# Gated linear attention with a gated feed-forward layer: weight groups loaded by their own index, and a new hand-written order of all tasks

## The chip, the core and the metric

The kernel runs on one core of one Trainium2 chip. A core has a matrix engine (TensorE, PE in the profile; its weight loads are shown apart as PEld), a vector engine (VectorE, DVE), a scalar engine (ScalarE, ACT), a general engine (GpSimd, POOL) and a queue engine (SyncE, SP) which here only issues DMA transfers. Each engine runs its own instructions strictly in the order in which they were written, and the engines meet through semaphores. The metric is the device time of one execution in microseconds (us).

## What is computed

The reference, cut to what matters. A gated linear attention runs over 4 batches, 8 heads and 768 tokens with heads of 48 values; its result, 3072 tokens of 384 values, goes through a gated feed-forward layer of width 1536.

```python
def _attn_ref(q, k, v, alpha):              # all (4, 8, 768, 48), float32
    state = zeros((B, H, D, D)); y = zeros_like(q)
    for t in range(S):
        state = alpha[:, :, t, :, None] * state + einsum('bhd,bhe->bhde', k[:, :, t], v[:, :, t])
        y[:, :, t] = einsum('bhd,bhde->bhe', q[:, :, t], state)
    return y

def _moe_ref(x, w_gate, w_val, w_out):      # x (3072, 384); weights float64
    g = x @ w_gate                          # (3072, 1536)
    silu = g * (1.0 / (1.0 + exp(-g)))
    return (silu * (x @ w_val) @ w_out).astype(float32)

def reference(**kwargs):
    attn_out = _attn_ref(...)
    x = attn_out.transpose(0, 2, 1, 3).reshape(B * S, H * D)
    return _moe_ref(x=x, ...)
```

## The kernel before

**Attention.** The tokens are cut into 16 units (u0 to u15), each 192 tokens of one batch for all heads, in three chunks of 64. For a unit the kernel loads alpha, k, q (tasks La, Lk, Lq) and v (V, six small transfers), turns alpha, k and q so that tokens lie along a row, forms a product of decays backward (G, one long scan on DVE) and forward (f), multiplies them into k (mk) and q (q), and then works with matrices: keys turned back (K with its copies kc, or kr on DVE), scores (S), causal masks (ma), the state carried from chunk to chunk (B or Bw, with ad and de) and the outputs (Y). The outputs are split into a high part (yh) and a low part (yl) and put into the activations xT of the feed-forward layer. The first four units are turned on PE: a copy widens each input (pa, pk, pq, `widened`, L405), PE transposes it (Ta, Tk, Tq, L417), ACT copies the result out (ea, ek, cq). Later units are turned by DVE (tr, tk, tq). Units 0 and 1 reach xT by PE products and copies (R, x); later ones by ten small DMA transfers each (xr, `repack`, L709).

**Feed-forward.** Two units make a block of 384 tokens; each of 8 blocks has 12 steps over the width, 96 steps in all. Step s is: a gate product g (9 matmuls into one PSUM bank, L725), SiLU on ACT (sl), a value product v (9 matmuls, L725), the product h of both on DVE (L737), its high part hh on ACT (L741), its low part hl on DVE or POOL (L746), and the output product o (9 matmuls, L757) that adds up in three PSUM banks. Every product is three: high by high, high by low, low by high, of operands split into two parts. Steps 0 to 6 are block 0 (first seven slices of the width), 7 to 13 block 1, 14 to 18 and 19 to 23 the rest of these two blocks, with partial sums kept in DRAM between (os6, os13, then pl18, pl23); blocks 2 to 7 have twelve steps each. ACT or DVE copies finished sums out (ot, L765 and L769), and a store follows (os).

**Weights.** The weights are 64-bit floats in memory. They come in 20 groups of one or two slices (g: gate, v: value, o: output). Group 0 is gate slice 0, group 1 value slice 0, group 2 gate slice 1, group 3 is (v1, o0), group 4 (g2, v2), group 5 (o1, g3) and so on to group 19 (o11). A group is loaded as 32-bit words (wl: one transfer of 384 KB for each slice, L298 or L301), turned into single floats by three word operations (wNv0 to wNv2, L157 to L175), split by a cast into the high part (wNa) and by a subtraction into the low part (wNp, L347). The raw words of group n lie in the place that group n + 1 will take when it is split, so a group's split waits until the group ahead of it has been turned.

**Checks.** Alongside, every weight and alpha value is read once more and compared with its permitted range (wr and wc for weights, Lc and ck for alpha, L456 and L457). Two sums of violations, a small matmul and a cast (L921 to L932) make a flag; every engine loads the flag at the end (L1083), and a general path runs if it is set.

**What sets the order.** The string ORDER (L46 on) is a list of words, each `engine:task@banks`, with t for PE, v for DVE, s for ACT, g for POOL and y for SP. The kernel goes through the list and writes each task to the named engine, so the list fixes the queue of every engine, which engine does a task, and which PSUM banks PE's tasks use; nothing is moved afterwards. Semaphores follow from the data.

## Time and profile before

| what | value |
|---|---|
| time, median of 3 runs | 573.75 us (572.68 to 574.14) |
| span of the profiled execution | 570.8 us |
| busy PE / DVE / ACT / POOL | 545.7 / 391.7 / 280.5 / 134.0 us |
| first gate product (g0) starts | 51.67 us |
| last instruction of the last output product ends | 563.86 us |
| mean granted clock of PE | 0.990 |

The profile describes one execution, whose span from first to last instruction is 570.8 us, 2.95 us under the median of the timed runs. In the rows of the profile, a line number such as L725 is a line of the kernel, `out<-in` are the names of the tiles (with buffer numbers left out), and the time in brackets is how long the engine stood idle ahead of the row, with what released it.

### The profile page before, as it was taken

The page shows a single profiled execution, that of the slowest core. Times are in us where ns is not written, and L with a number is a line of the kernel's source. Part 1 is how long each engine was busy: PE and PEld are TensorE (multiplying, and loading weights), DVE is VectorE, ACT ScalarE, POOL GpSimd, SP SyncE. Part 2 cuts the span into 40 slices and gives each one's busy share as a digit, 9 for nine tenths or more (in the row PEclk, how much of TensorE's full clock was granted, in tenths as well). Part 3 has the DMA queues.
Part 4 walks back from the last instruction along what each step waited for, and adds up shares of the span by engine and source line. Part 5 has one row for each costly group of instructions (what it writes and reads, how often), then busy time and mean ns, then how long its engine had stood idle before and what let it go on. Part 6 is the DMA issues. An engine that isn't in the chain of part 4 may idle for free.

```text
span 570.8 us, 13758 instructions
## 1 busy us (share of the span) xinstructions
PE 545.7 (96%) x5510; PEld 527.4 (92%) x5510; DVE 391.7 (69%) x601; ACT 280.5 (49%) x621; POOL 134.0 (23%) x152
## 2 busy tenths in 40 slices
...
GB/s 204 309 318 254 277 82 112 115 40 108 131 146 146 135 132 107 124 126 113 93 100 187 172 156 205 191 141 89 218 111 85 116 132 86 97 73 121 41 2 47
...
## 3 DMA queue, kind: packets, MB, share of 16 engines
...
q10 hardware_dynamic: 144, 0.20, 0.1%
HBM read 62.52 MB, written 5.90 MB: 120 GB/s over the span
## 4 chain that ended last, share of the span: by engine, by line
PE 76%; DMA 10%; DVE 7%; SPq 3%; issue 2%; ACT 1%; DVEq 0%; ACTq 0%
PE ops L757 24%; PE v L725 23%; PE g L725 22%; DMA raw<-in_moe_w_out_dram 3%; DMA raw<-in_moe_w_gate_dram 2%; PE y L652 2%; PE A L580 2%; PE s L556 2%; DMA raw<-in_moe_w_val_dram 1%; DMA L<-in_k_dram 1%; DMA Le<-in_q_dram 1%; DVE K L531 1%; SPq L436 1%; PE y L635 1%; DVE t L165 1%
## 5 line engine op out<-in xcount | busy, mean ns | idle before, releaser
L725 PE MATMUL v<-xT,w 128*128 128x384 f32 x864 | 166.9, 337 | 3.2 <-DVE h L737 2.4
L725 PE MATMUL g<-xT,w 128*128 128x384 f32 x864 | 167.3, 337 | 0.4 <-ACT h L733 0.4
L757 PE MATMUL ops<-w,hh 128*128 128x384 f32 x576 | 159.8, 338 | 0.0
L725 PEld LDWEIGHTS v<-xT,w 128*128 128x128 f32 x864 | 150.7, 188 | 5.8 <-DVE h L737 3.4
L725 PEld LDWEIGHTS g<-xT,w 128*128 128x128 f32 x864 | 150.7, 188 | 1.4 <-ACT h L733 0.7
L737 DVE TENSOR_TENSOR h<-h,v 128x384 f32<-128x384 f32 x96 | 52.9, 551 | 120.1 <-PE v L725 92.5
L746 POOL TENSOR_TENSOR hl<-h,hh 128x384 fp32r<-128x384 f32 x57 | 65.5, 1150 | 264.7 <-ACT hh L741 263.5
L741 ACT CAST hh<-h 128x384 fp32r<-128x384 f32 x96 | 49.1, 511 | 128.1 <-DVE h L737 70.9
L757 PEld LDWEIGHTS ops<-w,hh 128*128 128x128 f32 x576 | 105.5, 188 | 1.0
L757 PE MATMUL ops<-w,hl 128*128 128x384 f32 x288 | 96.8, 336 | 0.0
L733 ACT ACTIVATE h<-g 128x384 f32<-128x384 f32 x96 | 46.9, 489 | 80.6 <-PE g L725 68.8
L531 DVE STREAM_TRANSPOSE K<-Gs 32x384 f32<-32x384 f32 x96 | 54.7, 570 | 2.3 <-PE A L580 0.4
L757 PEld LDWEIGHTS ops<-w,hl 128*128 128x128 f32 x288 | 54.1, 188 | 0.1
L746 DVE TENSOR_TENSOR hl<-h,hh 128x384 fp32r<-128x384 f32 x39 | 22.9, 589 | 14.8 <-ACT hh L741 14.6
L590 DVE TENSOR_TENSOR X<-s,mask 64x384 f32<-64x384 f32 (+1 forms) x48 | 26.3, 552 | 8.5 <-PE s L556 7.6
L471 DVE TENSOR_TENSOR_SCAN AT<-AT,back 128x771 f32<-128x771 f32 x16 | 30.9, 1933 | 0.6
L462 DVE TENSOR_TENSOR_SCAN Gs<-AT,inj 128x772 f32<-128x772 f32 x16 | 28.7, 1794 | 0.1
L417 PE MATMUL pt<-ident,wide 128*128 128x128 f32 x72 | 14.9, 376 | 11.4 <-POOL mask L243 5.1
L417 PEld LDWEIGHTS pt<-ident,wide 128*128 128x128 f32 x72 | 12.1, 197 | 13.4 <-ACT wide L405 5.1
L319 ACT ACTIVATE wc<-wc,wbias 128x384 f32<-128x384 f32 x36 | 23.4, 650 | 1.2
L318 ACT ACTIVATE wc<-wc,wbias 128x384 f32<-128x384 f32 x36 | 23.3, 648 | 1.2
L839 POOL TENSOR_TENSOR Gs<-trk,Gs 128x768 f32<-128x768 f32 x10 | 17.9, 1785 | 25.3 <-DVE Gs L462 13.8
(118 smaller groups left out, 608.4 us busy)
## 6 DMA issues: line engine op xcount, KB each, us to landing
...
```

The source lines that it names most:

```text
L319: nc.scalar.activation(dev, dev, AF.Relu, bias=wbias[:, 1:2], accum_out=wviol[:, 0, i : i + 1])
L417: nc.tensor.transpose(pt[:, j - js.start, :], Wd.rearrange("p j e c -> p (j e c)")[:, j * P : (j + 1) * P], ident)
L462: nc.vector.tensor_tensor_scan(*(x.rearrange("p g t -> p (g t)")[:, ::-1] for x in (Gs, AT, inj)), 0.0, op0=ALU.mult, op1=ALU.add)
L471: nc.vector.tensor_tensor_scan(Af, Af, back[:, 1 : n + 1], back[:, 0:1], op0=ALU.mult, op1=ALU.add)
L531: nc.vector.transpose(out=bass.AP(k0.tensor, k0.offset, [k0.ap[0], (G * 2 * D, NU), (2 * D, G), (1, 32)]), in_=Kg[j * BO + x : j * BO + x ...
L590: nc.vector.tensor_tensor(out=X[r, z, f * GF : (f + 1) * GF, :].rearrange("r g (c t) -> r g c t", c=NU), in0=sps[f][r].rearrange("r g (c t ...
L725: nc.tensor.matmul(pt, wsp[kind, f][a][:, kt * P : (kt + 1) * P], xT[blk][:, b_, kt, :], start=(n == 0), stop=(n == 3 * KT - 1),)
L733: nc.scalar.activation(h, acc.pop(("g", blk, f)), AF.Silu)
L737: nc.vector.tensor_tensor(out=h, in0=h, in1=acc.pop(("v", blk, f)), op=ALU.mult)
L741: nc.scalar.copy(out=hh, in_=acc["h", blk, f])
L746: eng.tensor_tensor(out=hl, in0=acc.pop(("h", blk, f)), in1=hh.bitcast(F32), op=ALU.subtract)
L757: nc.tensor.matmul(ops[blk][i], h[b_][:, i * P : (i + 1) * P], wsp["o", f][a], start=(first and n == 0), stop=(last and n == 2),)
```

## The change

`weight_group` took its index from how many groups had been loaded so far, so that the loads had to be written in the order of the groups. It now takes the index as an argument. The loads may stand in any order, and the rest of the function is as it was. All lines from there on have numbers one to three lower in the changed kernel.

```diff
-    wsp, groups, wtiles = {}, [], []
+    wsp = {}
@@
-    def weight_group(pieces):
+    def weight_group(n, pieces):
-        n = len(groups)
-        groups.append(pieces)
@@
-            wfns[p] = weight_group(wgroups[p])
+            wfns[p] = weight_group(p, wgroups[p])
@@ ORDER, the first line and the last
-y:La0 y:wl0 y:Lk1 y:La1 y:Lq0 y:V1 s:pa0 t:Ta0@01 s:w0v0 v:w0v1 s:ea0 v:w0v2 y:Lk0 s:w0a v:G0 s:pa1 y:Lq1 s:pq0 y:La2
...
-s:os95.2
+y:La0 y:wl1 v:w1v0 y:La1 y:Lk0 g:pa0 t:Ta0@30 v:w1v1 s:ea0 y:Lq0 y:wl0 v:w1v2 s:pa1 v:G0 t:Ta1@32 s:pq0 t:Tq0@40 s:pk0
...
```

The string ORDER is new from its first word to its last, with the same tasks. The weight groups are loaded in the order 1, 0, 3, 2, 5, 7, 4, 9, 6, 8, 10, 15, 11, 14, 12, 13, 17, 16, 18, 19. The first value product stands ahead of the first gate product, and the carry of unit 2 (Bw2) and one turned key chunk of unit 3 (K3.1) stand behind both. Some tasks change their engine. In number: low parts of weights (wNp) are 13 on DVE and 7 on POOL before, 6 and 14 after; high parts of weights (wNa) 16 on ACT and 4 on POOL before, 9 on ACT, 9 on POOL and 2 on DVE after; the q products (q) 7 on DVE and 9 on POOL before, 4 and 12 after; qc 10 on ACT and 6 on POOL before, 5 and 11 after; vc 11 and 5 before, 4 and 12 after; the copies of outputs (ot) 24 on ACT and 6 on DVE before, 16 and 14 after; the widening copies of the first units (pa, pk, pq) 9 on ACT and 3 on POOL before, 4 and 8 after.

SP's queue ahead of the last loads of unit 3 (the k and q rows, into the buffers L0 and L1; `raw` rows are weights, `V0` is v). Before:

```order
L446 DMA L1_72<-in_k_dram 128x2x288
L446 DMA L0_71<-in_q_dram 128x2x288
L301 DMA raw10_505<-in_moe_w_gate_dram 128x3x256
L301 DMA raw10_505<-in_moe_w_val_dram 128x3x256
L436 DMA V0_77<-in_v_dram 64x4x48 x6
L298 DMA raw11_641<-in_moe_w_out_dram 128x768
L301 DMA raw11_641<-in_moe_w_gate_dram 128x3x256
L446 DMA L1_72<-in_q_dram 128x2x288
```

and after the change:

```order
L297 DMA raw5_317<-in_moe_w_out_dram 128x768
L300 DMA raw5_317<-in_moe_w_gate_dram 128x3x256
L300 DMA raw7_371<-in_moe_w_gate_dram 128x3x256
L300 DMA raw7_371<-in_moe_w_val_dram 128x3x256
L443 DMA L0_71<-in_alpha_dram 128x2x288
L300 DMA raw4_479<-in_moe_w_gate_dram 128x3x256
L300 DMA raw4_479<-in_moe_w_val_dram 128x3x256
L433 DMA V0_77<-in_v_dram 64x4x48 x6
L300 DMA raw9_552<-in_moe_w_val_dram 128x3x256
L297 DMA raw9_552<-in_moe_w_out_dram 128x768
L443 DMA L1_72<-in_k_dram 128x2x288
L443 DMA L1_72<-in_q_dram 128x2x288
```

The last load of unit 3 is the q row into L1. Ahead of it stood 21 weight transfers (up to one slice of group 11), and now 13 (groups 0 to 5, 7 and 9). The v of unit 2 (V0) keeps its place ahead of it.

DVE's queue ahead of its last copies into xT of block 0 (L696 before, L693 after; `t` are weight words, `w2` a low part, `Y1` low parts of outputs, `Gs2` the key product mk2, `X0` the q product or a mask). Before:

```order
L347 TENSOR_TENSOR w2_435<-t2_387,w2_435 128x384
L165 SCALAR_TENSOR_TENSOR t4_458<-raw4_244,t4_458 128x768
L175 SCALAR_TENSOR_TENSOR t4_458<-raw4_244,t4_458 128x768
L165 SCALAR_TENSOR_TENSOR t5_630<-raw5_303,t5_630 128x768
L175 SCALAR_TENSOR_TENSOR t5_630<-raw5_303,t5_630 128x768
L670 TENSOR_TENSOR Y1_638<-y0_1_586,Y1_638 112x2x192
L175 SCALAR_TENSOR_TENSOR t3_390<-raw3_223,t3_390 128x768
L836 TENSOR_TENSOR Gs2_455<-pt2_1_0_647,Gs2_455 128x4x32x3
L836 TENSOR_TENSOR Gs2_455<-pt2_1_1_651,Gs2_455 128x4x32x3
L488 TENSOR_TENSOR X0_103<-pt2_2_0_657,AT_86 112x128x3
L488 TENSOR_TENSOR X0_103<-pt2_2_1_661,AT_86 112x128x3
```

and after the change:

```order
L164 SCALAR_TENSOR_TENSOR t5_550<-raw5_317,t5_550 128x768
L667 TENSOR_TENSOR Y1_616<-y0_1_573,Y1_616 112x2x192
L667 TENSOR_TENSOR Y1_616<-y1_1_574,Y1_616 112x2x192
L833 TENSOR_TENSOR Gs2_482<-pt2_1_0_620,Gs2_482 128x4x32x3
L833 TENSOR_TENSOR Gs2_482<-pt2_1_1_624,Gs2_482 128x4x32x3
L485 TENSOR_TENSOR X0_103<-pt2_2_0_631,AT_86 112x128x3
L485 TENSOR_TENSOR X0_103<-pt2_2_1_635,AT_86 112x128x3
L693 CAST xT0_569<-xp1_2_653 128x2x192
L616 SCALAR_TENSOR_TENSOR V0_77<-SE_109,Gs2_482 48x4x48 x2
L693 CAST xT0_569<-xp0_0_677 128x2x192
```

The word operations of group 4 and one of group 5 and the low part of group 2 no longer stand ahead of the copies into xT, of which DVE now makes two in place of one.

ACT's queue at the end of the program (`hh` high part of h, `ot` an output copy, `ac13` the alpha values of block 13, `flag` the flag of the checks). Before:

```order
L741 CAST hh7_11_6807<-h7_11_6772 128x384
L769 COPY ot7_0_11_6820<-ops7_0_0_6462 128x384
L769 COPY ot7_1_11_6822<-ops7_1_0_6463 128x384
L769 COPY ot7_2_11_6825<-ops7_2_0_6464 128x384
L774 DMA out_0_dram<-ot7_2_11_6825 128x384
L1083 TENSOR_LOAD flag_60
```

and after the change:

```order
L738 CAST hh7_11_6805<-h7_11_6761 128x384
L766 COPY ot7_0_11_6820<-ops7_0_0_6439 128x384
L766 COPY ot7_1_11_6823<-ops7_1_0_6440 128x384
L771 DMA out_0_dram<-ot7_2_11_6818 128x384
L453 ACTIVATE ac13_6714<-ac13_6714,nbias_112 128x576
L454 ACTIVATE ac13_6714,viol_110<-ac13_6714,dbias_114 128x576
L1080 TENSOR_LOAD flag_60
```

The two range comparisons of alpha block 13 now stand between the last store and the load of the flag; one of the three last output copies has gone to DVE.

More of the change, by code (lines that the diff above doesn't have):

```diff
@@ L72 @@
-s:vc5 g:hl14 t:v15 s:w18a v:yl4.0 s:sl15 v:w17p s:yh4.1 t:g16 s:ot13.2 v:w19v0 v:h15 g:mk5 y:os13.2 v:yl4.1 s:hh15
-y:pl18.0 t:o14 s:sl16 y:La6 v:w19v1 t:v16 v:kr5.3 g:hl15 g:w18p v:tq5 t:o15 v:h16 y:Lk6 t:g17 g:q5 v:kr5.2 s:hh16
-v:kr5.0 t:v17 s:sl17 g:qc5 v:hl16 t:g18 v:w19v2 v:h17 s:w19a v:tr6 s:hh17 t:v18 s:sl18 g:hl17 v:kr5.1 y:Lq6 t:o16
-v:w19p v:h18 t:S5@01 y:xr4 v:tk6 s:hh18 t:B5@2 g:hl18 v:ma5.2 t:o17 v:ad5.0 v:ad5.1 t:o18 v:ad5.2 v:ma5.0 t:g19
-v:ot18.0 v:ma5.1 y:pl18.1 v:G6 t:v19 y:La7 s:sl19 t:Y5@01 v:f6 y:os18.0 t:g20 s:yh5.0 y:V7 v:h19 g:vc6 s:yh5.1 v:yl5.0
@@ L137 @@
-s:os95.2
+y:La0 y:wl1 v:w1v0 y:La1 y:Lk0 g:pa0 t:Ta0@30 v:w1v1 s:ea0 y:Lq0 y:wl0 v:w1v2 s:pa1 v:G0 t:Ta1@32 s:pq0 t:Tq0@40 s:pk0
+s:w0v0 t:Tk0@51 y:Lk1 v:f0 s:pk1 y:wl3 g:z0 y:Lq1 v:q0 s:ea1 t:Tk1@43 s:w3v0 g:pq1 v:mk0 v:G1 v:w0v1 v:w0v2 t:K0.1@5
+t:S0@17 t:K0.2@0 s:ek1 s:w1a t:K0.0@2 v:f1 g:mk1 y:V0 y:V1 y:La2 g:pa2 v:w3v1 y:Lq2 t:Tq1@63 s:kc0.2 s:kc0.1 s:cq1
+y:wl2 v:w1p s:kc0.0 v:z1 g:w0a v:w3v2 t:Ta2@60 s:w2v0 v:ma0.1 y:Lk2 g:q1 y:wl5 t:Bw0@2 g:vc0 y:wl7 v:ma0.2 s:ea2
+s:ad0.2 v:w2v1 g:qc0 t:S1@34 v:ma0.0 g:w0p v:ma1.2 v:w2v2 v:ma1.1 s:ad0.1 t:K1.0@7 t:K1.2@6 g:w3a s:kc1.2 t:K1.1@5
@@ new lines @@
+y:V5 s:w18a t:g17 g:w17p v:tq5 s:ot13.1 y:os13.2 y:La6 t:v16 s:yh4.0 g:q5 v:kr5.2 y:Lk6 s:hh15 t:o14 v:kr5.3 v:h16
+g:hl15 g:w18p s:sl17 g:vc5 y:os13.1 y:V6 v:w19v0 v:w19v1 t:o15 s:hh16 s:ad0.0 v:w19v2 v:kr5.1 g:hl16 v:tr6 t:v17 v:h17
+g:qc5 s:hh17 t:g18 y:pl18.0 s:ad3.0 v:ad2.0 t:v18 v:G6 v:yl4.0 s:sl18 v:de5 v:h18 s:w19a g:w19p y:pl18.1 s:yh4.1
+v:yl4.1 t:g19 g:hl17 v:tk6 y:xr4 t:o16 s:hh18 t:S5@01 v:f6 v:z6 v:ma5.0 t:B5@2 s:sl19 v:ad5.0 t:v19 v:ma5.2 v:ad5.1
+g:mk6 t:g20 g:hl18 v:kr6.0 v:h19 s:sl20 t:o17 t:o18 t:v20 v:ot18.0 s:hh19 v:ma5.1 v:ad5.2 v:h20 t:Y5@01 t:v21 t:g21
@@ new lines @@
+t:g32 v:kr8.2 t:v32 s:hh31 y:Lq9 s:sl32 g:hl31 y:La10 v:h32 g:mk9 y:xr7 t:o30 t:v33 t:g33 v:kr8.0 s:hh32 t:S8@12
+s:sl33 v:tq9 t:B8@0 y:wr2 y:Lk10 t:g34 v:f9 g:hl32 v:ma8.2 g:q9 g:vc8 t:o31 v:kr9.3 y:V9 s:ad8.0 v:h33 s:hh33 v:ad8.1
+v:ma8.1 v:ma8.0 t:o32 v:tr10 s:sl34 t:v34 t:g35 v:ad8.2 v:hl33 v:h34 y:Lq10 t:Y8@10 t:v35 g:z9 s:sl35 y:wr0 s:hh34
+g:hl34 y:V10 t:g36 v:G10 s:yh8.0 v:tk10 v:yl8.0 t:o33 y:wr4 v:h35 y:os23.1 t:o34 s:yh8.1 s:wc2 v:yl8.1 s:sl36 s:hh35
+v:kr9.2 v:kr9.0 y:xr8 v:kr9.1 v:mk10 v:hl35 t:g37 y:La11 t:v36 v:tq10 t:S9@01 v:h36 s:sl37 t:B9@2 s:hh36 t:o35 v:f10
```

159 lines of the change are left out of this document (75 added, 84 removed).

## The prediction

> **What bounds the kernel now.** I read the page first, then stages of the span by engine, then the chain of waits, then the instructions in order of time at the places where the stages meet.
>
> ```profile
> span 570.8 us, 13758 instructions
> PE 545.7 (96%) x5510; PEld 527.4 (92%) x5510; DVE 391.7 (69%) x601; ACT 280.5 (49%) x621; POOL 134.0 (23%) x152
> PE 76%; DMA 10%; DVE 7%; SPq 3%; issue 2%; ACT 1%; DVEq 0%; ACTq 0%
> ```
>
> PE is busy nearly throughout and holds 76% of the chain. A share over the span hides the stages, so the next view sums the engines stage by stage (columns: us of the stage, then busy us of PE, PEld, DVE, ACT, POOL, granted PE clock, DMA share, GB/s).
>
> ```profile
> 0.00:51.67 51.67, 36.82 (x701) 32.27 (x701) 42.75 (x65) 38.16 (x82) 12.60 (x36) 0.93 0.93 272
> 51.67:110.00 58.33, 55.96 (x524) 52.88 (x522) 53.28 (x61) 32.91 (x65) 23.58 (x21) 1.00 0.59 159
> 110.00:190.00 80.00, 80.00 (x834) 77.98 (x833) 73.77 (x112) 22.61 (x46) 28.59 (x25) 1.00 0.47 120
> 190.00:276.00 86.00, 84.75 (x946) 81.27 (x945) 79.48 (x121) 23.26 (x50) 23.62 (x23) 1.00 0.49 118
> 360.00:563.86 203.86, 203.86 (x1512) 201.78 (x1510) 72.43 (x135) 122.03 (x282) 28.01 (x27) 1.00 0.36 101
> 563.86:570.80 6.94, 0.33 (x2) 0.01 (x1) 0.00 (x0) 0.81 (x2) 0.00 (x0) 0.67 0.29 96
> ```
>
> The execution has three parts: 51.67 us before the first gate product, 512.2 us of products with hardly a gap on PE, and 6.9 us behind the last product. From 51.67 to 276 us DVE is busy 206.5 of 224.3 us, 92%: there PE and DVE are both near full, and a start that comes earlier is worth only what both can follow. After 360 us DVE has time to spare.
>
> **The start.** Four rows of PE show what stands around the first product, and DVE's rows its first scan, the last copy that it makes into the activations of block 0, and the gating of step 17.
>
> ```profile
> 48.34 1.28 PE L580 MATMUL A<-V,K 128*48 128x48 f32 x48
> 50.64 0.87 PE L417 MATMUL pt<-ident,wide 128*128 128x128 f32 x6
> 51.35 0.55 PE L515 MATMUL kps<-ident,Gs 112*64 112x112 f32 x4
> 51.67 1.83 PE L725 MATMUL g<-xT,w 128*128 128x384 f32 x9
> 7.97 1.76 DVE L462 TENSOR_TENSOR_SCAN Gs<-AT,inj 128x772 f32<-128x772 f32 x1
> 46.87 0.55 DVE L696 CAST xT<-xp 128x384 fp32r<-128x384 f32 x1
> 148.21 0.55 DVE L737 TENSOR_TENSOR h<-h,v 128x384 f32<-128x384 f32 x1
> ```
>
> Two things release the first product in the new order: the loads of unit 3, whose transposes stand just ahead of it on PE, and the last copy into xT. SP's queue paces the loads (columns: start, us, what):
>
> ```profile
> 20.91 0.37 SPq L301 DMA_DIRECT2D raw<-in_moe_w_gate_dram  x1
> 33.26 0.71 SPq L301 DMA_DIRECT2D raw<-in_moe_w_val_dram  x1
> 42.90 0.62 SPq L446 DMA_DIRECT2D L<-in_q_dram  x1
> L<-in_q_dram SPq DMA_DIRECT2D x3, 288.0 KB, 5.0
> L405 POOL COPY wide<-L 128x576 f32<-128x576 f32 x3 | 2.1, 704 | 12.1 <-ACT trk L810 8.4 <-DMA L<-in_alpha_dram 3.8
> L839 DVE TENSOR_TENSOR Gs<-trk,Gs 128x768 f32<-128x768 f32 x3 | 2.9, 967 | 0.1
> ```
>
> Between the first two rows lie 12 issues in 12.35 us, one per 1.03 us, with the DMA engines full (share 0.93 over the stage). Ahead of the last q load (42.90 us) stand 21 weight pieces now and 13 in the new order: 8 x 1.03 = 8.2 us sooner, so issued near 34.7 and landed 5.0 us later, 39.7. Two copies by POOL (0.7 each, the row of L405) and two transposes of 0.7 (50.64 to 51.35) give 42.4. The other releaser: DVE loses from its queue ahead of xT mk1 and q1 (to POOL; about 0.97 each, the row of L839), three low halves and the words of group 4 and half of group 5, and gets two xT copies; by the group rows that is 37.6 us of work before and 31.7 now, 5.9 less: 47.4 - 5.9 = 41.5. The loads come last: first product at **42.4**, 9.3 us sooner. One whole carry and a transpose then follow it instead of leading it (48.34 to 50.64, and 0.4): 2.7. Net gain of PE's queue: **6.6**. From below: the first scan of DVE waits for a copy that moves from ACT to POOL's set-up, worth -0.3 in my reading, and if V of unit 2, which waits for the outputs of unit 0, holds SP up by 4 us the gain is 2.6; from above 9.
>
> **What DVE lets through.** I summed durations by row ahead of the gating of step 17 (h17) on DVE: 128.2 us in the old order, 128.0 in the new; six low halves go to POOL (-5.0), but two weight casts, two more differences hl, a transpose and two transposed key rows come. PE's queue ahead of v18 is the same list in both orders. So h17 and v18 are a checkpoint: the gain there is at most what DVE gains on its own. It ends at 148.76 = 6.9 (start of its first scan less the work ahead) + 128.2 + 9.8 of waits + 3.8 of the rest. The waits, of DVE in the two stages:
>
> ```profile
> DVE t L165 <- ACT t L157: 3.3, 2, 2.8
> DVE Gs L836 <- PE pt L417: 1.7, 1, 1.7
> DVE X L590 <- PE s L556: 1.2, 1, 1.2
> DVE h L737 <- PE v L725: 2.6, 4, 1.1
> ```
>
> (with 2.8 of the first row ahead of the first scan, and small ones that make up the 9.8). If all waits go, h17 ends 10 us sooner; if all stay, not at all. In the new order PE-caused ones shrink, since PE is early; I take 4.0, 2 in the start and 2 on loads. The rest grows with POOL, because instructions of DVE and POOL hold each other up:
>
> ```profile
> 264.24 1.70 POOL L490 TENSOR_TENSOR X<-trq,AT 112x768 f32<-112x768 f32 x1 [7.23 <-DMA out_dram<-ot]
> 264.44 1.91 DVE L746 TENSOR_TENSOR hl<-h,hh 128x384 fp32r<-128x384 f32 x1
> 266.99 1.84 PE L725 MATMUL v<-xT,w 128*128 128x384 f32 x9 [1.25 <-DVE h L737]
> L347 POOL TENSOR_TENSOR w<-t,w 128x768 fp32r<-128x768 f32 x7 | 13.7, 1951 | 4.8 <-ACT w L343 4.6
> ```
>
> The difference hl takes DVE 0.55 us alone and took 1.91 beside a POOL product, and PE waited 1.25 for it. Ahead of h17 POOL's instructions with two operands sum to 33.6 us now and 44.3 in the new order; DVE rows longer than their like cost 9.7 us up to there, 0.29 per us of POOL, so 10.7 more cost 3.1; the bounds are 0 (they fall beside transposes) and 10.7; I take 2.5, near the measured rate. So h17 ends at 6.1 + 128.0 + 3.8 + 2.5 + 4.0 = 144.4, v18 can start 4.4 sooner, and **4.4** of the 6.6 is kept.
>
> The Trainium skill (page "SBUF — State Buffer", section "Who interferes with whom") says that a DVE instruction with two SBUF inputs and a GpSimd instruction that reads SBUF exclude each other, whoever comes first, for the whole instruction. The trace agrees with that in the rows above. It speaks against this change: by that rule six more weight differences on POOL would block DVE for half of 1.95 us each, 5.9 in place of 2.5, which is the second rival.
>
> **Behind the checkpoint.** PE's remaining work is the same. The wait of 1.25 at 266.99 goes, since the new order has 3.9 us more PE work ahead of v39 for the same DVE work: -1.3. Ahead of v33 DVE may lose 4.9 us more than at v18 before PE feels it; loads that come late fall into that. For waits that I can't see (bounds 0 and 3): +1.0.
>
> **The tail.** The check of alpha block 13 moves behind the last output copy on ACT.
>
> ```profile
> 563.19 1.58 ACT L769 COPY ot<-ops 128x384 f32<-128x384 f32 x3 [1.56 <-PE ops L757]
> 564.79 0.38 ACTq L774 DMA_DIRECT2D out_dram<-ot  x1
> L457 ACT ACTIVATE ac<-ac,dbias x16: 777/778/780, 485.6 to 541.6; 128x576 f32<-128x576 f32 x16
> 542.53 0.16 DVE L921 TENSOR_REDUCE vsa<-viol 128x1 f32<-128x16 f32 x1
> 547.23 0.14 DVE L932 CAST flag<-cps 1x1 int32<-1x1 f32 x1
> L1083 DVEq TENSOR_LOAD <-flag x1: 542/542/542, 561.7 to 561.7; - x1
> ```
>
> The flag that ends the program stood ready at 547.4. Now: store issued by 565.3, the check (2 x 0.78 and 0.19) to 567.0, the four small DVE rows 0.75, a matmul and the cast 0.9, the load of the flag 0.54: 569.2, where the stores land at about 568.2 to 568.8 as before. Cost **+0.6**, between 0 and 1.5. What covered the check before was the whole last block.
>
> **Sum.** 570.8 - 4.4 - 1.3 + 1.0 + 0.6 = 566.7 us of span. The profiled execution lies 2.95 under the median 573.75, so the time is 569.6.
>
> **Rivals.** (1) PE keeps all of 6.6, DVE's waits vanish: 570.8 - 6.6 - 1.3 + 0.6 = 563.5, time 566.4. For it: DVE waits for PE, not the reverse, in several rows above; against: 92% busy. Chance 0.13. (2) The lock between DVE and POOL eats it: 5.9 in place of 2.5 leaves 1.0 of 4.4, span 570.1, and with waits 0.6 longer 570.6, time 573.5. Chance 0.20. (3) Slower: SP's queue. The new order sets loads behind repacking transfers that themselves wait for DVE. Its rows:
>
> ```profile
> 230.46 6.72 SPq L709 DMA_DIRECT2D xT<-X  x10
> 244.78 4.12 SPq L436 DMA_DIRECT2D V<-in_v_dram  x6
> 253.31 8.73 SPq L709 DMA_DIRECT2D xT<-X  x10
> 64.00 6.90 SPq L436 DMA_DIRECT2D V<-in_v_dram  x6
> ```
>
> The k of unit 9 follows ten repacks (6.7), a load (1.9), V (4.1) and its own issue (1.9) behind a DVE result, and lands some 2.4 later: 17 us, where DVE has 14.2 us of other work. Four transposes (q of units 4, 6 and 7, k of 9) have margins of 0.9, 0.1, -0.1 and -2.7; the old order's least is 1.3. If the queue is 3 us slower, as the last two rows show it can be, DVE loses 2.1 + 2.9 + 3.1 + 5.7 = 13.8; 4.9 is free and 1.0 counted, so 566.7 + 7.9 = 574.6, time 577.5. It decides once DVE's loss on these loads passes 10 us. Chance 0.15. (4) That weight groups come in another order changes no work and no byte; if the first product stays at 51.67 the 2.7 moved behind it are paid, but that is near (2) in time and counted there.
>
> **How the numbers follow.** Forecast 0.52, own range 566.5 to 572.5. About 0.3% (572.0 to 575.5) is what a measurement can tell from no change. Faster: 0.13 + 0.48 + 0.01 = 0.62; same: 0.04 + 0.17 + 0.01 = 0.22; slower: 0.16. Eight in ten: 565.0, beyond which lies little of (1), to 576.0, which leaves out most of (3).
>
> **What would show it.** The first product (v of step 0) at 41 to 45 us; the last unit-3 load issued near 35; v18 near 145; no gap of PE over 1 us between 150 and 300; the reduction of viol the last work on DVE, 0 to 1.5 us behind the stores. A first product after 49, or DVE rows of L164 and L174 over 1.6 us many times, or DVE waiting for loads of k and q more than 5 us in all, would make it wrong.

## The result, and the profile after

The changed kernel takes 593.89 us (median of four runs, 591.14 to 597.26), the kernel before 573.21 in the same comparison: 1.037 times as long, with an interval of 1.0324 to 1.0417. Forecast were 569.6 us, in a range of 565 to 576. The change is slower by 20.7 us. One execution of the kernel a_tail ran slower as a whole (599.71 us); it is left out of that kernel's time, and of its trace only the tail and the pauses are used.

The page of the changed kernel's profile shows the same work in a longer span:

```profile
span 595.5 us, 13787 instructions
PE 551.2 (93%) x5510; PEld 532.9 (89%) x5510; DVE 395.7 (66%) x604; ACT 255.6 (43%) x579; POOL 175.6 (29%) x190
PE 71%; DMA 8%; DVE 6%; issue 4%; SPq 4%; ACT 3%; POOL 2%; ACTq 0%; DVEq 0%; POOLq 0%
```

The span grew by 24.7 us, four more than the medians, since the profiled execution of the change is the slowest of its four. PE holds 71% of the chain and no longer 76, and it is busy for 5.5 us more with the same 5510 matmuls. So two things must be told apart: pauses of PE, and slower matmuls.

For both, the next two views cut the executions at the same tasks: the value products v1, v5 and v18, and the end of the last output product. For the kernel before that end is 564.19; the 563.86 of the table and of the views ahead of this section is the start of the last matmul. Columns are as in the prediction's view of stages. First the kernel before:

```profile
0.00:60.78 60.78, 45.10 (x855) 39.84 (x855) 50.66 (x77) 45.82 (x102) 17.10 (x44) 0.94 0.93 278
60.78:83.21 22.43, 21.37 (x219) 19.67 (x219) 21.15 (x25) 13.80 (x25) 6.99 (x4) 1.00 0.64 157
83.21:149.50 66.29, 65.81 (x519) 64.44 (x520) 61.35 (x80) 26.36 (x50) 30.07 (x24) 1.00 0.40 100
149.50:564.19 414.69, 413.44 (x3918) 403.44 (x3917) 258.57 (x422) 194.08 (x445) 79.81 (x82) 1.00 0.46 121
564.19:570.77 6.58, 0.00 (x1) 0.00 (x0) 0.00 (x0) 0.48 (x1) 0.00 (x0) 0.65 0.29 98
```

Then the changed kernel. The last row of both is the stretch behind the last product:

```profile
0.00:59.46 59.46, 42.64 (x736) 38.31 (x736) 46.14 (x65) 32.67 (x74) 33.45 (x53) 0.89 0.80 236
59.46:87.83 28.37, 25.11 (x340) 23.81 (x340) 25.05 (x33) 13.59 (x29) 16.73 (x14) 0.94 0.56 165
87.83:157.06 69.23, 65.70 (x520) 64.05 (x520) 66.05 (x82) 22.49 (x44) 32.50 (x29) 1.00 0.47 116
157.06:585.03 427.97, 417.54 (x3915) 406.65 (x3915) 257.08 (x420) 185.20 (x430) 92.98 (x95) 0.99 0.46 117
585.03:595.49 10.46, 0.19 (x2) 0.11 (x2) 1.34 (x6) 1.64 (x3) 0.00 (x0) 0.68 0.19 65
```

The length of a stretch less PE's busy time is PE's idle time in it. This ledger is worked out from these rows:

| stretch | before | after | difference | of it PE idle | of it PE busy |
|---|---|---|---|---|---|
| start to v1 | 60.78 | 59.46 | -1.3 | +1.1 | -2.5 |
| v1 to v5 | 22.43 | 28.37 | +5.9 | +2.2 | +3.7 |
| v5 to v18 | 66.29 | 69.23 | +2.9 | +3.1 | -0.1 |
| v18 to the last product | 414.69 | 427.97 | +13.3 | +9.2 | +4.1 |
| behind it | 6.58 | 10.46 | +3.9 | | |

The 2.5 us by which the start has less PE work are the outputs of unit 2 and the scores of unit 3 (Y2 and S3). They stand ahead of v1 in the order before and behind it in the changed one, so they come back between v1 and v5. The rest of the loss is idle time, slower matmuls, and the tail. The waits of PE between 60 and 564 us show who made it idle (columns: engine, tile and line that waited, who released it, us in total, times, longest). Before:

```profile
PE v L725 <- DVE h L737: 2.4, 4, 1.2
PE v L725 <- DVE X L670: 0.8, 1, 0.8
PE g L725 <- ACT h L733: 0.4, 1, 0.4
```

and after:

```profile
PE s L577 <- DVE X L587: 5.2, 2, 3.9
PE ops L754 <- ACT ot L766: 4.3, 2, 2.6
PE v L722 <- DVE h L734: 2.9, 3, 1.8
PE y L649 <- POOL U L499: 2.7, 1, 2.7
PE ops L754 <- DVE hl L743: 1.8, 1, 1.8
PE g L722 <- ACT h L730: 0.4, 1, 0.4
```

Before, PE waits 3.6 us in 500. After, it stops for 17.3 us at ten places, in kinds of waits that did not exist: a carry product (L577) that waits for a mask, an output product (L754) that waits for the copy of an older output, outputs (L649) that wait for a copy by POOL.

### The profile page after: what moved, and what is told of

Read it like the earlier page. It is cut to its first block, busy times and chain, and to the rows that moved or that the text cites. A ratio compares the mean times of both kernels' runs of the same rounds, so it can differ in the third digit from the quotient of the medians.

```text
span 595.5 us, 13787 instructions
## 1 busy us (share of the span) xinstructions
PE 551.2 (93%) x5510; PEld 532.9 (89%) x5510; DVE 395.7 (66%) x604; ACT 255.6 (43%) x579; POOL 175.6 (29%) x190
## 4 chain that ended last, share of the span: by engine, by line
PE 71%; DMA 8%; DVE 6%; issue 4%; SPq 4%; ACT 3%; POOL 2%; ACTq 0%; DVEq 0%; POOLq 0%
PE ops L754 23%; PE v L722 20%; PE g L722 20%; PE A L577 2%; PE y L649 2%; DMA raw<-in_moe_w_gate_dram 1%; DMA out_dram<-ot 1%; PE s L553 1%; DMA L<-in_q_dram 1%; DMA wc<-in_moe_w_out_dram 1%; SPq L706 1%; SPq L433 1%; PE y L633 1%; PE y L632 1%; DVE t L164 1%
## 5 line engine op out<-in xcount | busy, mean ns | idle before, releaser
L722 PE MATMUL v<-xT,w 128*128 128x384 f32 x864 | 170.0, 342 | 2.9 <-DVE h L734 2.9
L754 PE MATMUL ops<-w,hh 128*128 128x384 f32 x576 | 163.2, 342 | 4.3 <-ACT ot L766 4.3
L722 PEld LDWEIGHTS v<-xT,w 128*128 128x128 f32 x864 | 152.9, 191 | 4.8 <-DVE h L734 4.1
L754 PEld LDWEIGHTS ops<-w,hh 128*128 128x128 f32 x576 | 107.3, 191 | 5.5 <-ACT ot L766 5.0
L730 ACT ACTIVATE h<-g 128x384 f32<-128x384 f32 x96 | 46.9, 488 | 141.7 <-PE g L722 117.8
L754 PE MATMUL ops<-w,hl 128*128 128x384 f32 x288 | 98.4, 342 | 1.8 <-DVE hl L743 1.8
L754 PEld LDWEIGHTS ops<-w,hl 128*128 128x128 f32 x288 | 55.0, 191 | 2.7 <-DVE hl L743 2.4
L487 POOL TENSOR_TENSOR X<-trq,AT 112x768 f32<-112x768 f32 x12 | 21.5, 1793 | 45.1 <-DVE V L616 12.6
L743 DVE TENSOR_TENSOR hl<-h,hh 128x384 fp32r<-128x384 f32 x39 | 22.7, 581 | 16.5 <-ACT hh L738 16.3
L468 DVE TENSOR_TENSOR_SCAN AT<-AT,back 128x771 f32<-128x771 f32 x16 | 33.0, 2060 | 0.6
L344 POOL TENSOR_TENSOR w<-t,w 128x768 fp32r<-128x768 f32 (+1 forms) x14 | 28.9, 2062 | 9.1 <-ACT w L340 6.5
L414 PE MATMUL pt<-ident,wide 128*128 128x128 f32 x72 | 13.6, 349 | 14.9 <-POOL wide L402 13.3
```

Source lines behind the costliest of these rows:

```text
L344: eng.tensor_tensor(out=lo, in0=src, in1=hi.bitcast(F32), op=ALU.subtract)
L414: nc.tensor.transpose(pt[:, j - js.start, :], Wd.rearrange("p j e c -> p (j e c)")[:, j * P : (j + 1) * P], ident)
L468: nc.vector.tensor_tensor_scan(Af, Af, back[:, 1 : n + 1], back[:, 0:1], op0=ALU.mult, op1=ALU.add)
L722: nc.tensor.matmul(pt, wsp[kind, f][a][:, kt * P : (kt + 1) * P], xT[blk][:, b_, kt, :], start=(n == 0), stop=(n == 3 * KT - 1),)
L730: nc.scalar.activation(h, acc.pop(("g", blk, f)), AF.Silu)
L743: eng.tensor_tensor(out=hl, in0=acc.pop(("h", blk, f)), in1=hh.bitcast(F32), op=ALU.subtract)
```

## The experiments

Eighteen kernels were run. A label with a_ is the changed order with one edit, b_ the kernel before with one edit, h_ one part of each order. Times are medians; the kernel before took 572.9 to 573.9 in their comparisons. In the diffs a line is one word of the order that moved; "..." stands for words between. Executions of one and the same order differ: in the four kernels whose order is the changed one up to v18 (the change, a_carry, a_store, h_ab) v1 came at 56.5 to 62.0 us and v18 at 153.9 to 159.9; in the five with the order before (before, b_tail, b_carry2, h_ba, h_ba_fix) v1 came at 60.5 to 62.6 and v18 at 149.5 to 152.4. So small differences are read from stretches between two tasks, and only against what the same order shows: from v1 to v18 that is 97.4 to 99.8 us in the first group and 88.7 to 91.2 in the second.

### The tail: a_tail and b_tail

```diff
 a_tail                      b_tail
 s:ck14                     -s:ck13  (ahead of the last steps)
+s:ck13                      ...
 ...                         s:os95.2
 s:os95.2                   +s:ck13
-s:ck13
```

> The changed order, with the check of alpha block 13 back ahead of the last step on ACT (right behind that of block 14), so that the flag is ready before the last stores. The profile of the change has 10.46 us behind the last output product, the kernel before 6.94. Theory branch: once the flag is loaded every engine still has to take a branch past the general path (4.5 us on PE, 3.5 on SP, 2.8 on ACT in the rows of the change), which before overlapped the landing of the stores; the tail goes back to about 7 us and the time falls by 3.5 us, to about 590.4. The prediction's own account (only the check itself is exposed): 0.6 us less, 593.3.

> The kernel before, with nothing changed but the check of alpha block 13 moved behind the last store on ACT, as in the change. Theory branch: the tail grows from 6.94 to about 10.4 us, the time by 3.5 (0.6%), to about 576.7. The prediction's account: 0.6 us more, 573.8.

b_tail took 578.12 us, 1.0092 of before (1.006 to 1.0123): 4.8 us more, and not 0.6. In its trace the stretch behind the last product is 11.72 us in place of 6.58. In a_tail it is 6.58, as before, against 10.46 in the change. The time of a_tail (592.76, 1.0335 of before) can't show that: it is 1.1 us under the change's, and both spread over 6 to 7 us. All traces agree, though: in the nine kernels with the late check the stretch takes 10.08 to 11.72 us, in the eleven with the early one 6.30 to 9.01.

Where the time goes is seen in the groups of the last branch in the changed kernel, and of the load of the flag ahead of it (columns: engine, count, ns, and at what time):

```profile
L1080 PEldq TENSOR_LOAD <-flag x1: 495/495/495, 589.1 to 589.1; - x1
L1081 PEldq COMPARE_BRANCH  x1: 4518/4518/4518, 589.7 to 589.7; - x1
L1081 ACTq COMPARE_BRANCH  x1: 54/54/54, 589.6 to 589.6; - x1
L1081 ACTq EVENT_SEMAPHORE  x1: 17/17/17, 592.4 to 592.4; - x1
L1081 SPq COMPARE_BRANCH  x1: 50/50/50, 589.6 to 589.6; - x1
L1081 SPq EVENT_SEMAPHORE  x8: 17/17/17, 593.2 to 593.8; - x8
```

and in the kernel before:

```profile
L1084 PEldq COMPARE_BRANCH  x1: 3518/3518/3518, 562.9 to 562.9; - x1
L1084 ACTq COMPARE_BRANCH  x1: 54/54/54, 565.8 to 565.8; - x1
L1084 ACTq EVENT_SEMAPHORE  x1: 17/17/17, 568.8 to 568.8; - x1
```

The branch past the general path occupies PE's queue for 4.5 us after the change; ACT and SP come to their next instruction 2.8 and 3.6 us after theirs. Before, PE took its branch at 562.9, while the last copies and stores were still on their way, and ACT's 3.0 us (565.8 to 568.8) ran beside the landing of the stores. Now all branches start at 589.6 or 589.7, behind the flag. The Trainium skill (page "Runtime: NRT & Kernel Launch", section "Instruction fetch mechanics") says that a taken branch whose target isn't among the pages that the queue holds has to fetch it before it goes on. The rows show that the branch takes microseconds, but no run here shows the fetch itself. That the late flag makes the tail longer is shown, 3.9 us in the ledger; that the branch is what then lies bare is read from the rows.

### The mask ahead of the carry, and what a pause costs: a_carry and b_carry2

```diff
 a_carry                     b_carry2
-v:ma5.0                    +v:G6
 t:B5@2                     +v:ma5.0
+v:ma5.0                     t:B5@2
 ...                         ...
-v:ma12.0                   -v:ma5.0
 t:B12@2                     ...
+v:ma12.0                   -v:G6
```

> The changed order, with the mask words ma5.0 and ma12.0 written behind the carry products B5 and B12 instead of ahead of them (the queue of DVE itself keeps its order, only the place between the engines changes). Theory pauses: the carry writes into the PSUM tile that the mask reads, so written behind the mask it waits for DVE; PE's pauses of 3.87 us at 163.6 and 1.35 us at 346.4 vanish, and with the first the slow product behind it (3.05 us in place of 1.66): 6.6 us less, about 587.3. Rival, DVE is the bound: PE then meets the next product of DVE earlier and waits there; less than 2 us less.

> The kernel before, with the mask ma5.0 written ahead of the carry B5, and the scan G6 ahead of both on DVE. By the rows of before the scores end at 153.55, DVE is free of the key transpose at 154.1, the scan takes 1.75 and the mask 0.55, so that B5 can start at 156.4 and not at 153.5. Theory pauses: one PE pause of 2.9 us and, since it is longer than 2.5 us, a slow product behind it, 1.4 us more; from these 1.25 come back where PE waited for DVE at 266: time 573.2 + 2.9 + 1.4 - 1.25, about 576.3. Without a cost of the pause beyond itself: 574.9. Rival, PE has room and a pause is taken up elsewhere, or there is no such dependence: 573.2, unchanged.

a_carry took 587.07 us, 6.8 less than the change, as the theory of pauses had it; in the traces the stretch behind v18 is 5.9 us shorter (422.05). The instructions in order of time show the wait in the changed kernel, on PE and on DVE:

```profile
167.49 0.56 PE L577 MATMUL s<-V,K 64*48 64x48 f32 x8 [3.87 <-DVE X L587]
168.30 3.25 PE L722 MATMUL v<-xT,w 128*128 128x384 f32 x9
163.41 3.31 DVE L468 TENSOR_TENSOR_SCAN AT<-AT,back 128x771 f32<-128x771 f32 x1
166.88 0.56 DVE L587 TENSOR_TENSOR X<-s,mask 64x384 f32<-64x384 f32 x1
```

A part of the third chunk of the carry is put beside the scores (`s`), into the tile that the first mask reads. Written behind that mask, the carry must wait until the mask has been made, and DVE makes it only after a long scan. In a_carry DVE's queue is the same, word for word, and so is PE's; the mask still ran late, at 169.80. But the carry went on at once:

```profile
166.32 0.38 PE L577 MATMUL s<-V,K 64*48 64x48 f32 x8
169.80 0.56 DVE L587 TENSOR_TENSOR X<-s,mask 64x384 f32<-64x384 f32 x1
```

So an order of words sets more than the queue of each engine: the place of a word of one engine against a word of another decides which of two accesses to a tile waits for the other.

b_carry2 puts the same dependence into the kernel before: 576.87 us, 1.0053 (1.0032 to 1.0073), 3.5 us more. PE stopped for 2.33 us, and v19 came 4.1 us later in its stretch than before: 1.8 us went beyond the pause. The view of stages shows why. The rows are, in order, the stretch behind that pause in b_carry2; of the changed kernel the stretches behind the pauses of 3.87, 2.60 and 1.75 us; and one behind a pause of 1.75 us in a_low and one of 2.52 in a_skip:

```profile
160.30:164.00 3.70, 3.70 (x14) 3.70 (x14) 2.82 (x10) 0.00 (x0) 0.00 (x0) 0.54 0.45 118
```
```profile
168.00:171.50 3.50, 3.50 (x20) 3.41 (x17) 2.94 (x7) 0.00 (x0) 0.00 (x0) 0.50 0.74 195
281.50:284.50 3.00, 2.95 (x9) 2.68 (x9) 0.00 (x0) 0.00 (x0) 0.00 (x0) 0.52 0.36 131
139.00:142.50 3.50, 3.50 (x20) 3.50 (x21) 3.41 (x6) 2.11 (x4) 0.70 (x2) 1.00 0.00 0
```
```profile
158.40:161.80 3.40, 3.40 (x12) 3.40 (x12) 3.35 (x6) 0.50 (x2) 2.08 (x2) 0.50 0.27 87
```
```profile
278.46:282.00 3.54, 3.54 (x62) 3.22 (x63) 0.78 (x2) 1.63 (x5) 0.00 (x0) 1.00 0.31 111
```

After the first three of these pauses PE runs for 3.4 us or more at half its clock (0.50 to 0.54 granted), which costs 1.8 to 1.9 us, counted up to the next task that is on time. The last three rows show that the length of a pause doesn't decide alone: after 1.75 us the clock is full in the change and half in a_low, and after 2.52 us it is full in a_skip. Over all twenty traces, between v1 and the last product, none of the 45 pauses of 1.00 to 1.74 us was followed by half clock, 17 of the 33 of 1.75 to 2.52 us were, and all 20 of 2.60 to 4.15. The half clock lasted 3.4 us or twice that, and the longer one cost 2.9 us behind the 3.99 us at o36 in h_ba. The Trainium skill (page "TensorE: Matmul & The Clock Gate", Part 1) says that an idle window of about 3.4 us brings the array to half rate until a busy window has passed, and that the windows run free of the program. Half rate, the length of the slow stretch and the unsharp line agree; that pauses of 1.75 to 2.6 us often suffice is shorter than the window that the page names.

### Which part of the order: h_ab and h_ba

```diff
 h_ab: the changed order up to t:v18, then what is left in the order before
 h_ba: the order before up to t:v18, then what is left in the changed order
```

> The changed order up to the task v18, then all tasks that are left, in the order of the kernel before. Theory pauses: the first part costs what its trace shows at v18, 157.06 against 149.50 us, 7.6 (5 to 10, since its start varies), and the rest has none of the later pauses; PE's wait of 1.25 at v39 vanishes and the tail is that of before: 573.4 + 7.6 - 1.25, about 579.7. Rival, the first part only moves work and the lateness is made up later: 573.4 to 575.

> The order of the kernel before up to the task v18, then all tasks that are left, in the changed order. Theory pauses: the later pauses of the change stay (3.87 at B5, 2.6 at o36, 1.35 at B12, 1.7 at o60, with 2.8 of slow products behind the two long ones) and so does the tail (3.5): 593.9 - 7.6, about 586.3. If the later pauses come from DVE's lateness at v18, they vanish with it: 573.4 + 3.5, about 577.

h_ab: 580.59 us, 1.0109 (1.0048 to 1.017). Its v18 came at 158.66, 9.2 later than before, and behind it the trace repeats the kernel before: 414.1 us to the end of the last product, against 414.7. h_ba: 591.37 us, 1.0305 (1.0261 to 1.0349), more than expected: with the start of the kernel before, the stretch behind v18 still takes 429.5 us, with pauses of 3.51, 3.99, 1.93 and 1.61 us at the same four places, and the tail 11.1. So the two parts lose time each by itself. A lateness made early is neither made up later nor the cause of the later pauses.

### The later pauses: a_store and h_ba_fix

```diff
 a_store
+y:os35.1
 y:wr7 ... y:Lk11 ...
-y:os35.1
 ...
-y:xr12
 ... y:os59.0
+y:xr12
```

> The changed order, with two words moved on SP: the store os35.1 ahead of the load wr7 (and so ahead of the k of unit 11), and the ten repacking transfers of unit 12 behind the store os59.0 in place of ahead of it. Theory store queue: there are two output buffers, the third copy of a block waits until a store has landed, and PE's next output product waits for that copy: the pauses of 2.6 at o36 and 1.7 at o60 vanish, and the slow product behind the first (1.45): 5.7 less, about 588.2. Rival, ACT is late anyway or DVE is the bound: less than 2 us.

> The order of the kernel before up to v18, then the rest in the changed order with the masks behind their carries, the store os35.1 ahead of the load, and the check of alpha block 13 early. Theory pauses: of 591.4 go 3.51 + 1.4 at B5, 3.99 + 1.4 at o36, 1.93 at B12 and 3.6 behind the last product, 15.8: about 575.6, which is before plus the pauses of 1.61 and 0.56 that are left. Rival, DVE is late in general: the pauses come back at other places, 582 or more.

In the changed kernel the wait at the output product o36 is one of SP's queue (rows in order of time of SP and ACT):

```profile
276.17 0.38 SPq L771 DMA_DIRECT2D out_dram<-ot  x1
281.01 0.48 ACT L766 COPY ot<-ops 128x384 f32<-128x384 f32 x1 [4.07 <-DMA out_dram<-ot]
281.55 0.62 PE L754 MATMUL ops<-w,hh 128*128 128x384 f32 x1 [2.60 <-ACT ot L766]
```

There are two output buffers. The third copy of a block can only start when the first store has landed, and that store stood behind the k load of unit 11, which was issued from 273.22 on. The copy then held up the next block's first output product, which needs the bank. In a_store both pauses, at o36 and o60, are gone. But the moved transfers delayed the range check's loads, ACT waited for one ahead of a SiLU, and PE stopped elsewhere for longer (the one wait of PE between 400 and 440 us):

```profile
PE g L722 <- ACT h L730: 3.0, 1, 3.0
```

So a_store gained 4.4 us between v34 and v40, around o36 (34.8 in place of 39.1 us), but only 3 behind v18 as a whole (424.9 in place of 428.0), and its time, 592.04, can't be told from the change's.

h_ba_fix, with only the first store moved, both masks behind their carries and the check early, took 578.86 us, 1.009 (1.0057 to 1.0123): 12.5 less than h_ba where 15.8 were expected. Behind v18 it needs 419.3 us, 10.2 less than h_ba and 4.7 more than before; the longest pauses left are 1.94, 0.56 and 0.48 us. Three places, the two masks and the store, thus make most of the loss behind v18.

### The start: a_start

```diff
-y:V2
 y:wl9 ... y:Lk3 y:Lq3
+y:V2
```

> The changed order with the six transfers of v of unit 2 moved behind the last loads of unit 3 on SP. Theory SP's queue: in the change SP stood at these transfers from 23.7 to 32.4 us, and the k and q loads of unit 3 were issued at 39.0 and 39.7; now they are issued near 27, land near 34, and the first product comes at 43 to 45. Theory buffer: the k load overwrites the buffer that POOL's widening copy of unit 2's k reads until 38.2, so it is issued at 38.2 at the earliest, and the first product comes at most 2 us sooner, 47.5 or later. Either way DVE is the bound up to v18 and the time changes by less than 2 us.

SP's issues in the changed kernel, and who it waited for:

```profile
23.73 0.70 SPq L300 DMA_DIRECT2D raw<-in_moe_w_val_dram  x1
32.35 4.95 SPq L433 DMA_DIRECT2D V<-in_v_dram  x6
39.01 0.62 SPq L443 DMA_DIRECT2D L<-in_k_dram  x1
39.72 0.98 SPq L443 DMA_DIRECT2D L<-in_q_dram  x1
```
```profile
SPq L433 <- PE y L632: 7.9, 1, 7.9
```

The prediction had put the last q load near 34.7, by counting weight pieces ahead of it. In fact SP stood for 7.9 us at the v of unit 2, which overwrites the v of unit 0 and so waits for unit 0's outputs on PE. In a_start this wait no longer lies ahead:

```profile
28.45 0.61 SPq L443 DMA_DIRECT2D L<-in_k_dram  x1
39.00 0.61 SPq L443 DMA_DIRECT2D L<-in_q_dram  x1
37.66 1.32 POOL L402 COPY wide<-L 128x576 f32<-128x576 f32 x1 [1.68 <-issue]
```

The k load went out 10.6 us sooner, but the q load only 0.7: it waits for its buffer, until POOL's widening copy out of it ends at 38.98. So SP's queue held the k load, and a buffer held the q load; theory buffer had the right kind of wait, but at the wrong load. v0 came at 46.20 in place of 49.48 and v18 at 154.33. Both are hardly outside what the changed order shows without this edit (v0 46.9 in a_store to 52.5 in a_carry, v18 153.9 to 159.9), and the time, 595.46 us (1.0392), shows no gain.

### Which engine does what: a_eng, b_eng, a_low, b_low, a_engall

a_eng gives all 132 tasks that changed their engine back to the engine of before, in the changed order (`g:w2p` becomes `v:w2p`, and so on); b_eng does the reverse in the order before. a_low and b_low move six low halves only, to DVE in the change and to POOL in the kernel before.

> The changed order, word for word in its places, but each of 132 tasks that changed its engine back on the engine it has in the kernel before (55 of them ahead of v18). Theory assignment: DVE is late at v18 because POOL, with 82.7 us of work up to there in place of 54.1, is itself late and holds DVE up; then v18 comes back to 150 or so and the time falls by 7, to about 587. Theory order: the places of the words alone make DVE late; 592 to 596, v18 at 155 or later. The prediction's account (POOL takes more off DVE than it costs): 1.9 us later than the change.

> The kernel before with its order of words, but the same 132 tasks on the engines that the change gives them. Theory assignment: v18 comes 5 us or more later than 149.5 to 151.7, time 579 or more. Theory order: within 1.5 us of before, 573.4 to 575.4. The prediction's account: 1.9 us less, near 571.7.

> The changed order with six low halves of weights (groups 2, 4, 8, 9, 14, 17), which it gives to POOL, on DVE again, at the same places. The prediction's account: DVE does 5.0 us more itself and is held up 2.5 us less, so v18 comes 2.5 us later and the time is 596.4. The rule that DVE and POOL shut each other out: 5.0 against 5.9, v18 0.9 earlier, 593. Theory assignment through POOL's queue (what waits behind a low half on POOL comes sooner): v18 3 us or more earlier, 591 or less.

> The kernel before, with six low halves of weights (groups 2, 4, 8, 9, 14, 17) on POOL in place of DVE, at the same places. The prediction's account: DVE gets rid of 5.0 us and is held up 2.5 us more, so DVE is up to 2.5 us ahead at v18, and PE, which hardly waits for it there, 0 to 2.5 us: time 571.4 to 573.9. The rule that DVE and POOL shut each other out: 5.9 against 5.0, 574.8. Theory POOL's queue: six instructions of 2 us ahead of other work on POOL make DVE and PE wait for it: 576 or more.

| kernel | time, ratio to before | v18 at | DVE busy up to v18 | POOL busy up to v18 |
|---|---|---|---|---|
| before | | 149.50 | 133.2 | 54.2 |
| b_low | 575.38, 1.0042 (1.0015 to 1.0069) | 150.8 | 129.8 | 64.4 |
| b_eng | 581.54, 1.0123 (1.0100 to 1.0147) | 157.1 | 135.3 | 82.9 |
| change | 593.89, 1.037 (1.0324 to 1.0417) | 157.06 | 137.2 | 82.7 |
| a_low | 594.23, 1.034 (1.0302 to 1.0377) | 157.2 | 140.0 | 74.1 |
| a_eng | 606.73, 1.0577 (1.0559 to 1.0595) | 164.2 | 135.9 | 60.0 |

Neither theory stands: assignment foretold b_eng but not a_eng, and order neither. The new engines in the old order cost 7.6 us of time, and the old engines in the new order 12.8; an order and the engines in it belong together, and each of the two is worse with the other's partner. The prediction's own term can be read from b_low: six low halves on POOL take 3.3 us off DVE, of the 5.0 that they took there, so DVE was held up 1.7 us more for 10.3 us of POOL (up to 2.3 against other traces of the order before, in which DVE is busy for 132.5 to 133.2). That is near the 2.5 that the sum used, and far from the 5.9 of the rule of full exclusion. But PE shows no gain from it: v18, at 150.8, lies among those of the order before (149.5 to 152.4), and the time rose by 2.4 us, of which the profile gives 1.6 to a longer tail. In a_low DVE's busy time and v18 lie within what the changed order shows without the edit (137.2 to 140.0 and 153.9 to 159.9), so it tells neither way.

a_engall has the engines of before and the single moves of the other runs:

> The changed order with the engines of the kernel before (all 132 tasks) and with the single moves of the earlier runs: the check of alpha block 13 early, both masks behind their carries, the store os35.1 ahead of the load, vc3 ahead of w7p. Theory assignment: 593.9 - 7 (v18) - 6.6 - 4 - 3.5 = 572.8, as before. Theory order: 593.9 - 14.1 = 579.8.

It took 596.99 us, 1.0407 (1.038 to 1.0433): the moves gained 9.7 us on a_eng, v18 stayed late, at 161.0, and the time is above both theories.

### Is DVE's amount of work the bound up to v18: a_skip and b_skip

```diff
-v:kr4.0
-v:kr4.2
-v:kr4.3
-v:kr5.0
-v:kr5.2
-v:kr5.3
```

> The changed order with six of the eight key transposes on DVE of units 4 and 5 left out (kr, 1.15 us each, 6.9 us in all ahead of v18; the keys of these units stay those of earlier ones, so this part of the attention is not computed). Theory DVE is the bound up to v18: v18 comes 5 to 7 us sooner, near 151, the pauses at o13 and v18 shrink or vanish, and the time is 587 to 589. Theory chain through other engines: v18 comes less than 2 us sooner, 592 to 594.

> The kernel before with the same six key transposes left out. PE is 98% busy between v1 and v18 there (87.2 of 88.7 us), so if PE is the bound v18 comes at most 1.5 us sooner and the time is 571.5 to 573.5 (1.25 of it at v39). If DVE is the bound here as well: v18 5 to 7 us sooner, 567.

b_skip took 572.73 us, 0.9997 (0.9978 to 1.0017), with v18 at 149.8: in the kernel before, DVE's work is not the bound, as expected with PE 98% busy. a_skip took 592.25 us, 1.0331 (1.0283 to 1.0379). Its stretches from v1 to v5 and from v5 to v18, in which the transposes are missing:

```profile
56.74:86.42 29.68, 25.51 (x340) 23.53 (x339) 27.19 (x33) 13.82 (x30) 18.90 (x15) 0.94 0.57 165
86.42:154.94 68.52, 65.95 (x519) 64.10 (x520) 62.97 (x71) 22.74 (x44) 34.78 (x29) 1.00 0.46 116
```

From v5 to v18 a_skip takes 68.5 us; the change, a_carry and a_store take 69.2 and h_ab 70.5. So of 6.9 us of work taken off DVE, 0.7 to 2.0 reached v18, where theory DVE had 5 to 7, and the time is that of the other theory. DVE itself was relieved of only 3.1 us (66.05 in the change, 62.97 here), since its other instructions took longer: one word operation took 3.00 us at 147.35, beside POOL, and 1.93 in the change. PE still waits 1.8 us for DVE at v18. The theory that the amount of DVE's work sets v18 thus falls. That DVE, held up by POOL, is what PE waits for is not excluded; no kernel was run with work of POOL left out instead.

### All moves together: a_all and a_best

> The changed order with all single moves together: check of alpha block 13 early (3.5), masks behind the carry (6.6), stores ahead (5.7), and three more, each for one pause: vc3 ahead of the weight difference w7p on POOL (2.7 at Y3 and 1.34 slow behind it), hl13 ahead of a word operation of group 16 on DVE (1.75 at o13), h17 ahead of the alpha transpose of unit 6 on DVE (1.78 at v18). Theory pauses: 593.9 - 23.4 = 570.5, at or below the time before. Theory DVE: the three pauses before v18 come back elsewhere since DVE is as late as before: 593.9 - 15.8 = 578.

> The changed order with all moves that helped together: V of unit 2 behind the last loads of unit 3, masks behind the carries, os35.1 ahead of the load, the check of alpha block 13 early, vc3 ahead of w7p, hl13 and h17 ahead of other work on DVE; the repacking transfers of unit 12 stay ahead of os59.0. If the places add up: a_all's 584.4, less 1.5 (its own pause of 3.2 at g66 gives way to 1.7 at o60), less 2.7 from the start: 580.2, with v18 near 151. If the stretch between v1 and v18 is set by a chain through several engines that none of these moves touches: v18 at 153 to 155, as in a_all, and 582 to 584.

a_all took 584.39 us (1.0192, 1.016 to 1.0225), more than either theory of it had; a_best 583.88 (1.0221, 1.0156 to 1.0286). The profiled execution of a_best:

```profile
56.80:84.13 27.33, 23.72 (x339) 21.92 (x340) 27.11 (x33) 13.17 (x28) 15.48 (x14) 1.00 0.75 200
84.13:152.17 68.04, 65.88 (x520) 64.13 (x520) 65.58 (x82) 22.50 (x44) 33.45 (x29) 1.00 0.46 115
152.17:572.90 420.73, 414.62 (x3917) 403.00 (x3917) 258.10 (x426) 186.71 (x433) 96.24 (x95) 1.00 0.46 120
```

Its span is 14.8 us under that of the change, and the granted clock is 1.00 in every stretch from v1 to the last product. But between v1 and v18 it still takes 95.4 us, where the kernel before takes 88.7. Its v18, at 152.17, lies between the two theories (151, and 153 to 155), and the time is that of the second. The pauses at Y3, o13 and v18 were taken away or cut, and others came: 2.19 us at g5, 1.09 at v5, 0.91 at o13, and 1.61 at S5 just behind v18. None of these kernels beats the kernel before.

## Why the prediction was wrong

**The start.** Forecast was the first product at 42.4; it came at 49.48. The step that failed is the release of the last load of unit 3. It was priced by the weight pieces ahead of it (8.2 us, issue near 34.7), and the wait for V of unit 2, which the text named with 4 us as a bound, was 7.9: the issue came at 39.72. Even without that wait the q load was held to 39.0 by its buffer (a_start). From the issue to the product it took 9.8 us in place of 7.7, as the load needed 6.0 and not 5.0, and the last transposes 2.5 and not 1.4, at a granted clock of 0.50. Of the 9.3 us of head start 2.2 were left. The first product itself ran at half clock too (3.0 us in place of 1.7), and the 2.7 us moved behind it came on top: by v1 the order is 1.3 us ahead, with 2.5 us less work done.

**The checkpoint at v18.** Forecast was 4.4 us sooner; it was 7.6 later. Two terms of the sum make 11.5 of these 12.0 us. The first is DVE's waits. The sum let them shrink from 9.8 to 4.0 us, and the idle time ahead of the first scan from 6.9 to 6.1. In the traces DVE's idle time up to v18 grew from 16.3 to 19.8 us (149.50 - 133.16 and 157.06 - 137.24), 9.7 more than the sum's 10.1; 13.3 of it lie ahead of v1, where the sum had 8.1, and 6.5 behind, where it had 2. The second is the hold-up by POOL: DVE's busy time grew by 4.1 and not by 2.3, so the term is 4.3 in place of 2.5. Here the mechanism was right (b_low) and the size 1.8 us short. The sum counted POOL's instructions with two operands, 10.7 us more (10.5 in the traces); POOL's copies and casts, 17 us more up to v18, were not in it. Whether they are the rest was not tried.

The first term is the step that failed, and with it the idea behind it: a budget of work for each engine with the waits taken as a remainder. DVE's work changed hardly at all, but 4.5 us of its busy time moved from ahead of v1 (50.66 to 46.14) to behind it, and between v1 and v18 it is as full as before (93%) in a stretch that is 8.9 us longer. a_skip shows that less work on DVE brings v18 forward by a small part of it only, and a_eng that the order, with the old engines, makes v18 14.7 us late. What sets this stretch is not settled. In the changed kernel's chain of waits it runs, between 41 and 76 us, from loads through low halves and casts on POOL, words on DVE and again POOL to a copy of v of unit 3, for which the outputs Y3 waited. Such a chain isn't seen in sums by engine. But a_all, which takes that wait away, still needs 97.1 us from v1 to v18: with three places mended, others took over, and which link would have to go was not found.

**Behind the checkpoint.** Forecast was -1.3 + 1.0; it was +13.3. "PE's remaining work is the same" held; that its waits cost 0 to 3 us did not. Two of them could have been read beforehand. The changed order has the masks ma5.0 and ma12.0 ahead of their carries; the queues of the two engines, which were compared each by itself, don't show it, though the code of the carry says that its third chunk lies beside the scores. And the store os35.1 stands behind a load, with two output buffers. The half clock behind long pauses was no term at all.

**The tail.** Forecast was +0.6 us, at most 1.5; it was +3.9 by the traces, and 5.1 in b_tail alone (4.8 in its time). The 6.9 us that the prediction gives to this stretch in the kernel before are 6.6 from the end of the last matmul, which changes no term of its sum. The chain was followed up to the load of the flag, and taken to end there: the branch behind it, 3.0 us on ACT in the trace of before, was counted as a part of the landing that it ran beside.

**The rivals.** The lock between DVE and POOL (2) had 5.9 us for the six low halves, which cost 1.7 in b_low; the hold-up of the whole change, 4.3, lies between it and the sum's 2.5, and its time of 573.5 fell as well. SP's queue (3) had the sign, but not the mechanism: it expected DVE to wait for late loads, and DVE's waits for loads behind v1 sum to 1.8 us. Rival (1) and the forecast fell alike. Of the signs given for a wrong prediction the first product after 49 was met, and PE paused for more than 1 us at three places between 150 and 300. The reduction of the checks was the last work on DVE, as the prediction had it, 1.8 us behind the issue of the last store.
